# Regrouping the attention phases' exponentials: three pairs and four singles, with the PSUM banks handed out at build time

## The chip, the cores and the metric

The kernel runs on one core of a Trainium2 chip. Its engines work side by side, each through its own instructions in order: TensorE (PE) multiplies matrices into PSUM, ScalarE (ACT) computes exponentials and copies, VectorE (DVE) copies and adds, GpSimd (POOL) does small work in SBUF, and SP issues most of the DMAs. PSUM has eight banks of 128 x 512 float32; one matmul's result fills one bank. Semaphores order the engines where one needs what another has made, or where a buffer has to be free before it is written again.

The metric is the device time of one execution in microseconds, as the median of several runs. Separately, one execution was profiled instruction by instruction; times inside it are counted from its first instruction.

## What is computed

A sigmoid gate mixes two branches over one sequence of 2048 tokens and 512 channels: attention with 32 heads of 16 channels, and an MLP across the tokens.

```python
x = A_x
g = sigmoid((x * gate_w).sum(-1, keepdims=True))
# branch A: q, k, v = x @ wqkv in 32 heads of Dh = 16
scores = einsum("bhqd,bhkd->bhqk", q, k) * Dh ** -0.5
p = softmax(scores, axis=-1)
a = einsum("bhqk,bhkd->bhqd", p, v)   # heads side by side, then @ wo
# branch B: token mixing
h = layernorm(x)
u = gelu(einsum("bsd,sf->bdf", h, w1) + b1)
b = einsum("bdf,fs->bds", u, w2) + b2  # transposed back
out = g * a + (1 - g) * b
```

## The kernel before

The kernel first projects and normalizes x and computes the MLP's first layer. Then come 128 attention phases (the loop over p from line 994), and a short end that applies the output projection to the last rows.

**A phase.** Two heads and half of the queries make a group; a group takes four phases. One phase computes 16 blocks of scores, each 128 keys by 512 queries (line 1067), numbered n = 0 to 15. Each block fills one PSUM bank and is then read once from it, in one of three ways:

- a *copied* block: VectorE copies it to SBUF (line 1089), into one of six places of a wide tile; when all six are there, ScalarE takes the exponential of the whole tile, 128 x 3072, in one instruction (line 1102);
- a *single*: ScalarE takes the exponential of the one bank (line 1093);
- a *pair*: ScalarE takes the exponential of two neighbouring banks, 128 x 1024, in one instruction (line 1031, in the function exps).

Before the change, blocks 1, 3, 5, 8, 14 and 15 are copied, 0, 2, 4, 6, 7 and 9 are singles, and (10, 11) and (12, 13) are pairs.

**The second half of a phase** multiplies the exponentials with V (apply_v, line 963; "AV" below): 64 matmuls that add up in one more bank. They take first the six copied blocks of the phase before (HELD, since their wide exponential comes late) and then the ten singles and paired blocks of this phase (TURNS). VectorE adds the bank to the group's sum in SBUF (line 985). The first phase of a group ends the group before in a bank of its own, and so uses two banks in turn.

**Work beside the scores.** A score uses 64 rows of the TensorE array. Beside the first n_b scores of a phase (14 in most phases, 12 in some) stands a matmul on the other 64 rows (line 1076): a part of the MLP's second layer, of late queries or of the output projection. The scores after n_b have none, and each two of them, on different rows, can run at the same time. The list head says on which rows a score runs.

**What sets the order.** Everything here is in a manual schedule: each engine's instructions run in the order in which the program issues them. So on TensorE all 16 scores of a phase stand ahead of its AV, and AV ahead of the next phase's scores. A matmul that waits for a bank holds back all that follows it on TensorE. The extra dependencies with the reason EARLY (lines 1095, 1103, 1113) are on earlier work, so that a later instruction has one engine less to wait for. Work that other parts insert on VectorE stands in the lists amid (issued at the second to last score, line 1082) and later (after the wide exponential, line 1118).

**Banks.** One bank is kept for the matmuls beside; seven are left for the scores and AV. Before the change, the function shares turns one "spare" bank number into an order of the seven. Scores 0 to 9 are written to one-bank tiles. Then the pool is closed and opened again in another cut: two pair tiles of two banks, two one-bank tiles for scores 14 and 15, and one for AV. AV's bank, share[2], is that of score 9, the last single.

Of the kernel before, what the change touches and what calls it, by code (L numbers as in the profile page):

```python
# [9 lines left out]
F32 = mybir.dt.float32  # L10
# [22 lines left out]
NB = 512  # L33
NQ = S // NB
VC = DH + 1
SCALE = DH**-0.5
# [24 lines left out]
def gated_mix(ctx: ExitStack, tc: tile.TileContext, a_x, a_wqkv, a_wo, b_w1, b_b1, b_w2, b_b2, gate_w, out):  # L61
    nc = tc.nc
# [115 lines left out]
    with tc.tile_pool(name="vp", bufs=1, side="right") as pool:  # L178
# [138 lines left out]
        e = pool.tile([P, NS], F32, name="e")  # L317
# [4 lines left out]
        y, t, w = (pool.tile([P, NS], F32, name=n) for n in "ytw")  # L322
# [103 lines left out]
    with tc.tile_pool(name="gl", bufs=2, side="right") as gl:  # L426
# [74 lines left out]
        for f0, cs in order.items():  # L501
            n = min(NB, F - f0) // P
# [32 lines left out]
    ptp = att_ctx.enter_context(tc.tile_pool(name="pt", bufs=2, reuse_waits="tile"))  # L535
# [45 lines left out]
    PHASES, NSC, BANKS = 4, 16, 7  # L581
    LAST = NG * PHASES - 1
# [257 lines left out]
    dense = {}  # L840
# [83 lines left out]
    def shares(n):  # L924

        for one in range(0, BANKS, 2):
            lows = [k for k in range(one)][::2] + [k for k in range(one + 1, BANKS)][::2]
            for third in lows:
                if n in (third, third + 1):
                    first, second = (low for low in lows if low != third)  # L930
                    return [first, first + 1, one, second, second + 1, 2 * third + 1 - n, n]


    def regions():
        return tc.tile_pool(name="ps_s", bufs=1, space=PSUM, reuse_waits="tile")

    sums, latest, evac_done = {}, {}, []

# [49 lines left out]

    engines = {getattr(mybir.EngineType, name) for name in ("PE", "Activation", "DVE", "Pool", "SP")}
    with tc.manual_schedule(engines=engines):  # L990
        held, fence, turn, spare = [], None, 0, 0
        landed.clear()

        for p in range(LAST + 1):
# [14 lines left out]
            n_b = len(beside)  # L1009
            half = slice(0, HALF) if second else slice(HALF, P)  # L1010

            head = [second if n < n_b else (second + NSC - 1 - n) % 2 for n in range(NSC)]
            if n_b == NSC - 2:
                head[-2:] = second, 1 - second
            else:
                head[-4:] = second, 1 - second, 1 - second, second
            in_turn = list(range(n_b)) + ([14, 15] if n_b == NSC - 2 else [12, 13, 15, 14])
            qbs = {}
            for a, b in TURNS + HELD:
                if head[a] == head[b]:  # L1020
# [3 lines left out]
                    qbs[zero], qbs[one] = turn, 1 - turn  # L1024
                    turn = 1 - turn

            def exps(n):
                pt = ptp.tile([P, 2, NB], F32, name="p2", bufs=len(TWO))
                where = [share[(j - BANKS) % BANKS] for j in (n - 1, n)]
                low = min(where)  # L1030
                pairs_done.append(nc.scalar.activation(pt, twos[low, low + 1], AF.Exp, scale=SCALE))  # L1031
                for j, k in zip((n - 1, n), where):
                    units[j] = *units[j][:3], pt[:, k - low, :]

            pairs_done = []
            evac = evp.tile([P, len(EVAC), NB], F32, name="pe")
            units = {}
            share = shares(spare)
            pool = regions()
            psum = pool.__enter__()  # L1040
            ones = [psum.tile([P, NB], F32, name=f"s{n}") for n in range(BANKS)]
            for n in in_turn:
                i, qb = head[n], qbs[n]
                c = at[i][qb]
                at[i][qb] += 1
                if n < TWO[0][0]:
                    if n >= BANKS:
                        ones[share[n - BANKS]] = psum.tile([P, NB], F32, name=f"s{share[n - BANKS]}")
                    s = ones[share[n % BANKS]]
                else:  # L1050
                    if n == TWO[0][0]:
                        pool.__exit__(None, None, None)
                        pool = regions()
                        psum = pool.__enter__()
                        twos = {}
                        for low in range(BANKS):
                            if low == share[2]:
                                av = psum.tile([P, NB], F32, name="av")
                            elif low in (share[0], share[1]):
                                twos[low] = psum.tile([P, NB], F32, name=f"u{low}")  # L1060
                            elif low not in twos:
                                two = psum.tile([P, 2, NB], F32, name=f"t{low}")
                                twos[low], twos[low + 1] = two[:, 0, :], two[:, 1, :]
                                twos[low, low + 1] = two
                    s = twos[share[(n - BANKS) % BANKS]]
                rows_i = slice(i * HALF, i * HALF + ROWS)
                nc.tensor.matmul(  # L1067
                    s,
                    kt[grp][rows_i, c * P : (c + 1) * P],
                    qt[grp][rows_i, qb * NB : (qb + 1) * NB],  # L1070
                    start=True,
                    stop=True,
                )
                if n < n_b:
                    ps, a, b, begin, last, done = beside[n]
                    mm = nc.tensor.matmul(ps, a[half], b[half], start=begin and not second, stop=last and bool(second))  # L1076
                    if n == 0 and fence is not None:
                        tc.add_manual_dep(mm.ins, fence.ins.name, SYNC, reason=REASON)
                    if n == n_b - 1:
                        fence = nc.gpsimd.memset(token, 0.0)  # L1080
                        tc.add_manual_dep(fence.ins, mm.ins.name, SYNC, reason=REASON)
                if n == in_turn[-2]:
                    if n_b and second and beside[-1][-1] in between:
                        between[beside[-1][-1]]()
                    for what, *args in amid.get(p, ()):
                        what(*args)
                if n in EVAC:
                    pt = evac[:, EVAC.index(n), :]
                    nc.vector.tensor_copy(pt, s)  # L1089
                    units[n] = i, c, qb, pt  # L1090
                elif n in SINGLE:
                    pt = ptp.tile([P, NB], F32, name="p1", bufs=len(SINGLE))
                    one = nc.scalar.activation(pt, s, AF.Exp, scale=SCALE)  # L1093
                    if n == SINGLE[-1] and p:
                        tc.add_manual_dep(one.ins, earlier.ins.name, SYNC, reason=EARLY)
                    units[n] = i, c, qb, pt
                else:
                    units[n] = i, c, qb, None
                    if n in (TWO[0][1], TWO[1][1]):
                        exps(n)  # L1100
            for x in ([evac] if p < LAST else [evac[:, :2, :], evac[:, 2:, :]]):
                done = nc.scalar.activation(x, x, AF.Exp, scale=SCALE)  # L1102
# [19 lines left out]
            spare = share[2]  # L1122
            if ph == 0:
                if held:
                    apply_v(av, grp - 1, held, final=True)
                    spare = share[3]
                    av = twos[spare]
                apply_v(av, grp, turns)
            elif p < LAST:
                apply_v(av, grp, held + turns, await_loads=ph == PHASES - 1)  # L1130
            else:
                ot = sums[grp]
                nc.vector.tensor_scalar_max(ot, ot, least[0])
                first_out = ps_dn.tile([P, D], F32, name="dn")

                def meanwhile():
                    for i, (a, b) in enumerate(o_matmuls(1, NH, 0, 3)):
                        nc.tensor.matmul(first_out, a, b, start=i == 0, stop=False)

                apply_v(av, grp, held + turns + now_held, final=True, between=meanwhile)  # L1140
                last_ot = ot
            pool.__exit__(None, None, None)
            held = now_held
            if ph == PHASES - 1:
                assert at == [[NS, NS], [NS, NS]]


    with (
# [162 lines left out]
```

## Time and profile before

| What | us |
|---|---|
| Median of 3 runs (1265.22 to 1266.12) | 1265.29 |
| Span of the profiled execution, first to last instruction | 1263.6 |
| VectorE busy | 851.3 |
| Starts of the first and the last wide exponential | 283.2 and 1227.4 |

The profiled execution's time is known by its span; the three runs stand 1.6 to 2.5 us above it, for what lies before the first and after the last profiled instruction.

A line of a timeline has the start, the duration, the engine, the line of the kernel, the operation, the tiles (written <- read), their shape and how many instructions it merges; in brackets stands how long the engine was idle before and what ended that. PEld is TensorE's loading of weights, which goes on beside its matmuls. A matmul's or an exponential's recorded duration includes latency that overlaps with the next one, so the time that an engine needs for one is read from the distance of the starts or of the ends of several.

### The profile page before, as it was taken

How to read it: one execution, taken by the hardware profiler on the slowest of the kernel's cores; microseconds unless marked ns; L12 is line 12 of the kernel's file. 1: busy time of each engine (PE TensorE's matmuls, PEld its weight loads, DVE VectorE, ACT ScalarE, POOL GpSimd, SP SyncE). 2: the span in 40 equal slices, each digit the busy share in tenths (PEclk: the TensorE clock that was granted, in tenths of full speed). 3: DMA queues.
4: the chain of work that ended last, by engine and by line, in shares of the span. 5: the costliest groups of instructions: out<-in, count | busy, mean ns of one | idle time of the engine just before them, and what ended most of it. 6: DMA issues, size and time to landing. Idle time of an engine off the chain costs nothing.

```text
span 1263.6 us, 32707 instructions
## 1 busy us (share of the span) xinstructions
PE 1255.3 (99%) x13342; PEld 828.5 (66%) x13342; DVE 851.3 (67%) x1562; ACT 1069.0 (85%) x1405; POOL 198.9 (16%) x316
## 2 busy tenths in 40 slices
PE   9999999999999999999999999999999999999997
PEld 7888888875666666666666666666666666666666
DVE  5675453178767676767677677776777677678883
ACT  4443343269999999999999999999999999999990
POOL 0220444461010101010101101111111111000000
PEclk9999999999999999999999999999999999999999
DMA  4799443243744444544344443443543442366611
GB/s 132 252 333 334 145 120 105 83 129 108 214 122 104 89 102 85 157 86 97 77 105 93 97 93 84 91 88 79 114 102 71 91 100 60 56 164 177 152 59 70
DMA packets 100555, 152.31 MB, mean 121 GB/s; under 512 B 17109, under 2 KB 56171, under 8 KB 96300
## 3 DMA queue, kind: packets, MB, share of 16 engines
q1 hardware_dynamic: 99820, 149.08, 45.9%
q8 instruction: 107, 1.75, 0.6%
q10 hardware_dynamic: 576, 1.05, 0.2%
q14 instruction: 52, 0.43, 0.1%
HBM read 105.39 MB, written 44.68 MB: 119 GB/s over the span
## 4 chain that ended last, share of the span: by engine, by line
PE 99%; ACT 1%; DVE 0%; issue 0%
PE av L963 31%; PE s L1067 22%; PE acc L424 12%; PE t L1067 9%; PE acc L75 8%; PE t L963 5%; PE dn L1076 4%; PE u L1067 3%; PE pa L1162 2%; PE acc L199 1%; PE acc L268 1%; PE acc L245 0%; ACT p L1093 0%; ACT pe L1102 0%; PE dn L1162 0%; PE pa L1192 0%
## 5 line engine op out<-in xcount | busy, mean ns | idle before, releaser
L1093 ACT ACTIVATE p<-s 128x512 f32<-128x512 f32 x768 | 412.4, 791 | 0.1
L1102 ACT ACTIVATE pe<-pe 128x3072 f32<-128x3072 f32 x129 | 381.7, 2961 | 0.0
L1067 PE MATMUL s<-qs,ks 64*128 64x512 f32 x1280 | 330.2, 400 | 0.6 <-ACT p L1093 0.6
L1089 DVE COPY pe<-s 128x512 f32<-128x512 f32 x512 | 318.2, 683 | 4.8 <-PE s L1067 1.1
L1067 PEld LDWEIGHTS s<-qs,ks 64*128 64x128 f32 x1280 | 225.6, 184 | 93.3 <-issue 45.3
L1031 ACT ACTIVATE p<-t 128x1024 f32<-128x1024 f32 x256 | 278.5, 1265 | 0.0
L963 PE MATMUL av<-p,v 128*32 128x256 f32 x3880 | 227.1, 379 | 0.0
L1089 DVE COPY pe<-u 128x512 f32<-128x512 f32 x256 | 164.9, 686 | 72.0 <-PE u L1067 72.0
L963 PE MATMUL av<-pe,v 128*32 128x256 f32 x3072 | 192.5, 383 | 0.0
L985 DVE TENSOR_TENSOR ot<-av,ot 128x512 f32<-128x512 f32 (+2 forms) x160 | 93.2, 583 | 142.3 <-PE av L963 141.0
L68 POOL TENSOR_TENSOR w_lo<-w_raw,w_hi 128x512 fp32r<-128x512 f32 (+1 forms) x128 | 153.1, 1203 | 197.3 <-ACT w_hi L67 100.3
L1076 PE MATMUL dn<-u_hi,w_hi 64*128 64x512 f32 x448 | 181.1, 404 | 0.0
L963 PEld LDWEIGHTS av<-p,v 128*32 128x32 f32 x3880 | 126.0, 110 | 83.3 <-ACT p L1093 0.2
L1076 PE MATMUL dn<-u_hi,w_lo 64*128 64x512 f32 x448 | 180.6, 403 | 0.0
L1076 PE MATMUL dn<-u_lo,w_hi 64*128 64x512 f32 x448 | 180.4, 403 | 0.0
L1067 PE MATMUL t<-qs,ks 64*128 64x512 f32 x512 | 142.2, 412 | 0.0
L963 PEld LDWEIGHTS av<-pe,v 128*32 128x32 f32 x3072 | 86.7, 109 | 82.1 <-ACT p L1093 37.8
L1080 POOL MEMSET token<- 1x1 f32 x128 | 11.4, 89 | 742.2 <-PE dn L1076 701.7
L67 ACT CAST w_hi<-w_raw 128x512 fp32r<-128x512 f32 (+1 forms) x67 | 38.0, 569 | 82.9 <-PE acc L424 63.1
L1067 PEld LDWEIGHTS t<-qs,ks 64*128 64x128 f32 x512 | 72.9, 184 | 51.0 <-ACT p L1093 49.5
L424 PE MATMUL acc<-h_hi,w_hi 128*128 128x512 f32 x224 | 87.9, 392 | 0.0
L424 PE MATMUL acc<-h_hi,w_lo 128*128 128x512 f32 x224 | 87.8, 392 | 0.0
(171 smaller groups left out, 1616.0 us busy)
## 6 DMA issues: line engine op xcount, KB each, us to landing
w_raw<-in_B_w_dram SPq DMA_DIRECT2D x96, 256.0 KB
ks<-kp SPq DMA_DIRECT2D x192, 128.0 KB
qs<-qp SPq DMA_DIRECT2D x256, 64.0 KB
kp<-pc SPq DMA_DIRECT2D x16, 512.0 KB
qp<-pc SPq DMA_DIRECT2D x8, 768.0 KB
qp<-row SPq DMA_DIRECT2D x24, 256.0 KB
v<-v SPq DMA_DIRECT2D x4, 1088.0 KB
x<-in_A_x_dram SPq DMA_DIRECT2D x16, 256.0 KB
```

The lines of the kernel that those rows point to most:

```text
L67: copy(hi, src)
L68: return sub(lo, src, hi.bitcast(F32), ALU.subtract)
L75: nc.tensor.matmul(ps, a, b, start=start and n == 0, stop=stop and n == last)
L424: nc.tensor.matmul(p, a, b, start=first and k == 0, stop=last and k == 2)
L963: mm = nc.tensor.matmul(av[32 * j : 32 * (j + 1), i * QC : (i + 1) * QC], vb[b][:, v_at : v_at + 32], pt[:, h * QC : (h + 1) * QC], start= ...
L985: latest["add"] = nc.vector.tensor_tensor(x, y, x, ALU.add)
L1031: pairs_done.append(nc.scalar.activation(pt, twos[low, low + 1], AF.Exp, scale=SCALE))
L1067: nc.tensor.matmul(s, kt[grp][rows_i, c * P : (c + 1) * P], qt[grp][rows_i, qb * NB : (qb + 1) * NB], start=True, stop=True,)
L1076: mm = nc.tensor.matmul(ps, a[half], b[half], start=begin and not second, stop=last and bool(second))
L1089: nc.vector.tensor_copy(pt, s)
L1093: one = nc.scalar.activation(pt, s, AF.Exp, scale=SCALE)
L1102: done = nc.scalar.activation(x, x, AF.Exp, scale=SCALE)
```

## The change

The 16 blocks are now described by a string, one letter a block: s for a single, e for a copied block, and a, b and c for the three pairs. Blocks 0, 6, 7 and 8 are singles, 1, 4, 5, 9, 12 and 13 are copied, and (2, 3), (10, 11) and (14, 15) are pairs. The lists TURNS and HELD follow from it. The scores are issued in the order of their numbers in all phases.

The seven banks are one tile, banks, for all phases, and every access takes a slice of it. Which bank a block and AV get is worked out when the program is built: given_out goes through the 128 phases with a time for when each bank becomes free, gives each single or copied block the bank that is free first, each pair the two neighbouring banks that are free first, and AV the bank that is free first after the 16 blocks. The pair's exponential reads banks[:, low : low + 2].

```diff
-    EVAC = 1, 3, 5, 8, 14, 15
-    SINGLE = 0, 2, 4, 6, 7, 9
-    TWO = (10, 11), (12, 13)
-    TURNS = [(0, 2), (4, 6), (7, 9), *TWO]
-    HELD = [(1, 3), (5, 8), (14, 15)]
...
+    KINDS = "seaaeesssebbeecc"
+    SINGLES = 4
+    EVAC = [n for n, kind in enumerate(KINDS) if kind == "e"]
+    SINGLE = [n for n, kind in enumerate(KINDS) if kind == "s"]
+    TWO = [tuple(n for n, kind in enumerate(KINDS) if kind == two) for two in sorted(set(KINDS) - {"e", "s"})]
...
+    def given_out():
+
+        free, vector, scalar, stream, load, wide = [0.0] * BANKS, 0.0, 0.0, 0.0, 0.0, 0.0
+        given = []
+
+        def first_free(spread=1, at=None):
+            ways = [b for b in range(BANKS + 1 - spread)] if at is None else [at]
+            best = min(ways, key=lambda b: (max(free[b : b + spread]), b))
+            when = max(free[best : best + spread])
+            free[best : best + spread] = [1e9] * spread
+            return best, when
+
+        for p in range(LAST + 1):
+            singles = len(dense.get(p // 2, ()))
+            bank, open_two, scored, readers = {}, {}, {}, {}
+            copied = []
+            for n, kind in enumerate(KINDS):
+                alone = n < singles or (n - singles) % 2 == 0
+                if kind in "es":
+                    bank[n], when = first_free()
+                elif kind not in open_two:
+                    bank[n], when = first_free(2)
+                    open_two[kind] = bank[n] + 1, when
+                else:
+                    bank[n], when = open_two[kind]
+                start = max(when + 0.05, stream, load) if alone else max(when + 0.05, begun)
+                load = 0.0
+                begun, stream = start, start + 0.2305
+                scored[n] = start + 0.44
+                if kind == "e":
+                    vector = max(vector + 0.6, scored[n] + 0.69)
+                    free[bank[n]] = vector
+                    copied.append(vector)
+                elif kind == "s":
+                    scalar = max(scalar + 0.488, scored[n] + 0.6)
+                    free[bank[n]] = readers[n] = scalar
+                elif kind in readers:
+                    scalar = max(scalar + 0.914, scored[n] + 1.02)
+                    free[bank[n] - 1 : bank[n] + 1] = [scalar] * 2
+                    readers[n] = scalar
+                else:
+                    readers[kind] = None
+            done = sorted([x for x in readers.values() if x] + [readers[two[1]] for two in TWO])
+            scalar = max(scalar, max(copied) + 0.25) + 0.4267 * len(EVAC) + 0.093
+            sums = [first_free()]
+            at = max(stream + 0.12, sums[0][1])
...
+            given.append(([bank[n] for n in range(NSC)], [b for b, _ in sums]))
+        return given
...
+        given = given_out()
...
+        banks = ps_s.tile([P, BANKS, NB], F32, name="banks")
...
-            head = [second if n < n_b else (second + NSC - 1 - n) % 2 for n in range(NSC)]
-            if n_b == NSC - 2:
-                head[-2:] = second, 1 - second
-            else:
-                head[-4:] = second, 1 - second, 1 - second, second
-            in_turn = list(range(n_b)) + ([14, 15] if n_b == NSC - 2 else [12, 13, 15, 14])
+            head = [second if n < n_b else (second + n - n_b) % 2 for n in range(NSC)]
...
+            bank, av_banks = given[p]
+
+            def exps(two):
                 pt = ptp.tile([P, 2, NB], F32, name="p2", bufs=len(TWO))
...
+                low = bank[two[0]]
+                assert bank[two[1]] == low + 1
+                pairs_done.append(nc.scalar.activation(pt, banks[:, low : low + 2], AF.Exp, scale=SCALE))
...
+            av = banks[:, av_banks[0]]
+            for n in range(NSC):
...
+                s = banks[:, bank[n]]
...
-                if n == in_turn[-2]:
+                if n == NSC - 2:
...
-                    pt = ptp.tile([P, NB], F32, name="p1", bufs=len(SINGLE))
+                    pt = ptp.tile([P, NB], F32, name="p1", bufs=SINGLES)
...
-            tc.add_manual_dep(done.ins, pairs_done[0].ins.name, SYNC, reason=EARLY)
+            tc.add_manual_dep(done.ins, pairs_done[-2].ins.name, SYNC, reason=EARLY)
             evac_done.append(done)
-            earlier = pairs_done[1]
+            earlier = pairs_done[-1]
```

The functions shares and regions, the pools opened and closed in every phase and the variable spare are gone. In the first phase of a group, av is banks[:, av_banks[1]] after the group before has ended.

More of the change, by code (lines that the diff above doesn't have):

```diff
@@ L916, in gated_mix @@
     token, mark = (out_pool.tile([1, 1], F32, name=name, bufs=1) for name in ("token", "mark"))
-    EVAC = 1, 3, 5, 8, 14, 15
-    SINGLE = 0, 2, 4, 6, 7, 9
-    TWO = (10, 11), (12, 13)
-    TURNS = [(0, 2), (4, 6), (7, 9), *TWO]
-    HELD = [(1, 3), (5, 8), (14, 15)]
[L924 to L931, printed above, removed]
@@ L934, in regions @@
-    def regions():
-        return tc.tile_pool(name="ps_s", bufs=1, space=PSUM, reuse_waits="tile")
+    KINDS = "seaaeesssebbeecc"
[3 more added lines that the diff above has]
+    TWO = [tuple(n for n, kind in enumerate(KINDS) if kind == two) for two in sorted(set(KINDS) - {"e", "s"})]
+    assert all(len(two) == 2 for two in TWO) and len(KINDS) == NSC
+    own = sorted([(n, n) for n in SINGLE] + [(two[1], n) for two in TWO for n in two])
@@ new lines, in gated_mix @@
+    own = [n for _, n in own]
+    kept = list(EVAC)
+    if len(own) % 2:
+        own.remove(SINGLE[-1])
+        kept.append(SINGLE[-1])
+    TURNS, HELD = ([(x[i], x[i + 1]) for i in range(0, len(x), 2)] for x in (own, kept))
+    def given_out():
[41 more added lines that the diff above has]
+            at = max(stream + 0.12, sums[0][1])
+            at += 0.2157 * 2 * len(HELD)
+            if p % PHASES == 0 and p:
+                free[sums[0][0]] = at + 1.1
+                sums.append(first_free())
+                at = max(at, sums[1][1])
+            for i in range(0, 2 * (len(done) // 2), 2):
+                at = max(at, done[i + 1] + 0.05) + 0.2157 * 2
+            vector = max(vector + 1.6, at + 1.0)
+            free[sums[-1][0]] = vector
+            load = at + 0.3
+            given.append(([bank[n] for n in range(NSC)], [b for b, _ in sums]))
+        return given
@@ L990, in gated_mix @@
     with tc.manual_schedule(engines=engines):
-        held, fence, turn, spare = [], None, 0, 0
+        held, fence, turn = [], None, 0
+        given = given_out()
+        scores_ctx = ExitStack()
+        ps_s = scores_ctx.enter_context(tc.tile_pool(name="ps_s", bufs=1, space=PSUM, reuse_waits="tile"))
+        banks = ps_s.tile([P, BANKS, NB], F32, name="banks")
         landed.clear()
@@ L1025, in gated_mix @@
                     turn = 1 - turn
-            def exps(n):
+            bank, av_banks = given[p]
+            def exps(two):
                 pt = ptp.tile([P, 2, NB], F32, name="p2", bufs=len(TWO))
[L1029 to L1033, printed above, removed]
+                low = bank[two[0]]
+                assert bank[two[1]] == low + 1
+                pairs_done.append(nc.scalar.activation(pt, banks[:, low : low + 2], AF.Exp, scale=SCALE))
+                for k, j in enumerate(two):
+                    units[j] = *units[j][:3], pt[:, k, :]
             pairs_done = []
@@ L1037, in gated_mix @@
             units = {}
[L1038 to L1042, printed above, removed]
+            av = banks[:, av_banks[0]]
+            for n in range(NSC):
                 i, qb = head[n], qbs[n]
@@ L1045, in gated_mix @@
                 at[i][qb] += 1
[L1046 to L1065, printed above, removed]
+                s = banks[:, bank[n]]
                 rows_i = slice(i * HALF, i * HALF + ROWS)
@@ L1098, in gated_mix @@
                     units[n] = i, c, qb, None
-                    if n in (TWO[0][1], TWO[1][1]):
-                        exps(n)
+                    for two in TWO:
+                        if n == two[1]:
+                            exps(two)
             for x in ([evac] if p < LAST else [evac[:, :2, :], evac[:, 2:, :]]):
                 done = nc.scalar.activation(x, x, AF.Exp, scale=SCALE)
-            tc.add_manual_dep(done.ins, pairs_done[0].ins.name, SYNC, reason=EARLY)
+            tc.add_manual_dep(done.ins, pairs_done[-2].ins.name, SYNC, reason=EARLY)
             evac_done.append(done)
-            earlier = pairs_done[1]
+            earlier = pairs_done[-1]
             if n_b and second and beside[-1][-1]:
@@ L1121, in gated_mix @@
             turns, now_held = ([tuple(units[n] for n in pair) for pair in pairs] for pairs in (TURNS, HELD))
-            spare = share[2]
             if ph == 0:
@@ L1125, in gated_mix @@
                     apply_v(av, grp - 1, held, final=True)
-                    spare = share[3]
-                    av = twos[spare]
+                    av = banks[:, av_banks[1]]
                 apply_v(av, grp, turns)
@@ L1141, in gated_mix @@
                 last_ot = ot
-            pool.__exit__(None, None, None)
             held = now_held
@@ L1145, in gated_mix @@
                 assert at == [[NS, NS], [NS, NS]]
+        scores_ctx.close()
     with (
```

## The prediction

> **What bounds the kernel now.** I read the page first, then ScalarE's timeline over one phase, then TensorE's over the same phase, then who waits for the single exponentials. The page (busy time by engine, tenths by slice, the chain that ended last):
>
> ```profile
> span 1263.6 us, 32707 instructions
> ...
> PE 1255.3 (99%) x13342; PEld 828.5 (66%) x13342; DVE 851.3 (67%) x1562; ACT 1069.0 (85%) x1405; POOL 198.9 (16%) x316
> ...
> ACT  4443343269999999999999999999999999999990
> ...
> PEclk9999999999999999999999999999999999999999
> ...
> PE 99%; ACT 1%; DVE 0%; issue 0%
> ```
>
> The chain names TensorE, but a busy PE is no proof: matmuls overlap. ScalarE is full from the ninth slice on, in the 128 attention phases. Its timeline over one phase (start, duration, count):
>
> ```profile
> 706.88 3.01 ACT L1102 ACTIVATE pe<-pe 128x3072 f32<-128x3072 f32 x1
> 709.58 3.25 ACT L1093 ACTIVATE p<-s 128x512 f32<-128x512 f32 x6
> 712.47 2.20 ACT L1031 ACTIVATE p<-t 128x1024 f32<-128x1024 f32 x2
> 714.31 3.00 ACT L1102 ACTIVATE pe<-pe 128x3072 f32<-128x3072 f32 x1
> 717.00 0.79 ACT L1093 ACTIVATE p<-s 128x512 f32<-128x512 f32 x1
> ```
>
> Starts run ahead of the work, so I go by ends. The wide exponential ends at 706.88+3.01 = 709.89, the six singles at 712.83, the two pairs at 714.67, the next wide one at 717.31. That is 2.94 for six singles (0.49 each), 1.84 for two pairs (0.92 each), 2.64 for the wide one: 7.42 us, with every instruction started before the last one ended. **ScalarE is saturated at 7.42 us a phase.** TensorE over the same phase:
>
> ```profile
> 709.05 0.50 PE L1067 MATMUL s<-qs,ks 64*128 64x512 f32 x1
> ...
> 709.39 0.39 PE L1067 MATMUL s<-qs,ks 64*128 64x512 f32 x1
> ...
> 711.23 0.39 PE L1067 MATMUL s<-qs,ks 64*128 64x512 f32 x1
> ...
> 712.47 0.42 PE L1067 MATMUL u<-qs,ks 64*128 64x512 f32 x2
> 712.88 1.50 PE L963 MATMUL av<-pe,v 128*32 128x256 f32 x24
> 714.20 2.34 PE L963 MATMUL av<-p,v 128*32 128x256 f32 x40
> 716.47 0.49 PE L1067 MATMUL s<-qs,ks 64*128 64x512 f32 x1
> ```
>
> The first score takes 0.34 us to the second; the next eight take (711.23-709.39)/8 = 0.23 each. The last two scores, with no other matmul beside them, start together, and the product with V ("AV") 0.41 later. AV to the next phase's first score: 716.47-712.88 = 3.59. So TensorE's own loop, if no bank is late, is 0.34 + 13 x 0.23 + 0.41 + 3.59 = 7.33: **only 0.09 below ScalarE**. And AV waits for a bank even now (who waited for L1093):
>
> ```profile
>   PEld av L963: 38.1, 128
> ```
>
> AV started 0.05 after the sixth single ended (712.88 against 712.83), and this row counts such a wait in all 128 phases. It costs nothing yet, because ScalarE's backlog covers it.
>
> **What the change takes away.** Two singles become one pair: 2 x 0.49 - 0.92 = 0.06 us a phase, 7.36 in place of 7.42, 7.7 us in 128 phases. Vector copies (six), matmuls, loads and stores stay as many; nothing is added to SP's or POOL's queue. Vector work inserted between copies now comes behind the sixth copy, with some 2.5 us until the AV sum needs VectorE; I cost it at nothing; without that cover it would cost its own length in the few phases that have it. A score into half of a pair no longer waits for both banks; that is counted below, bank by bank.
>
> **What it moves.** The order becomes s e a a e e s s s e b b e e c c (s single, e copied, a/b/c pairs). Scores 14 and 15, which were copied by VectorE, are now pair c and need two neighbouring banks; TensorE works in order, so AV stands behind them. I followed the function in the diff through its 128 phases for its bank numbers alone, taking no time from it. The later of c's two banks to come free was last read by: copy 9 with single 7 in 42 phases (class A), single 8 in 59 (class B), copy 12 in 27 (class C). Phase 67's banks are 3 6 1 2 4 5 0 3 6 4 1 2 0 5 3 4 (c in 3, 4: score 7's and 9's, class A); phase 69's 4 1 5 6 2 0 3 4 1 2 5 6 3 0 1 2 (c in 1, 2: score 8's, B); phase 68's 0 5 1 2 3 4 6 0 5 3 1 2 6 4 5 6 (c in 5, 6: 12's, C).
>
> How late are these? Latencies with no backlog come from the first phase, where ScalarE starts empty, and from a phase in which the last scores came late:
>
> ```profile
> 278.57 0.39 PE L1067 MATMUL s<-qs,ks 64*128 64x512 f32 x1
> ```
> ```profile
> 279.00 0.60 ACT L1093 ACTIVATE p<-s 128x512 f32<-128x512 f32 x1
> ```
> ```profile
> 709.81 2.49 DVE L1089 COPY pe<-s 128x512 f32<-128x512 f32 x4
> 712.92 1.29 DVE L1089 COPY pe<-u 128x512 f32<-128x512 f32 x2 [0.62 <-PE u L1067]
> ```
> ```profile
> 1119.37 1.28 DVE L1089 COPY pe<-s 128x512 f32<-128x512 f32 x2
> ...
> 1120.70 0.19 PEld L1067 LDWEIGHTS u<-qs,ks 64*128 64x128 f32 x2 [0.32 <-DVE pe L1089]
> ...
> 1121.13 0.84 PE L963 MATMUL av<-pe,v 128*32 128x256 f32 x10
> ```
> ```profile
> L1031 ACT ACTIVATE p<-t x256: 1068/1281/1325, 281.4 to 1225.6; 128x1024 f32<-128x1024 f32 x128
> ```
>
> A single ends 0.43 + 0.60 = 1.03 after its score starts. A pair with nothing queued is not shown. Its floor is 0.43 + 0.92 (its service) = 1.35; its ceiling 0.43 + 1.07 (the least of 256 rows, which still had a queue) = 1.50. I take 1.03 + (0.92-0.49) = 1.46, near the ceiling, because that row is a pair itself. A copy starts 709.81-709.39 = 0.42 after its score and takes 0.69, ending 1.11 after; the next copies follow at (2.49-0.69)/3 = 0.60. A score starts 0.05 after the bank's reader ends (1119.37+1.28 = 1120.65, then 1120.70), and after such a wait AV comes 0.43 after the last score (1121.13). That step has 0.23, a score's spacing, as its other end, and I take 0.43 because that row is the same situation.
>
> From a phase's first score (0): scores 1, 3, 4, 9 and 12 at 0.34, 0.80, 1.03, 2.19 and 2.88 (9 waits 0.01 for copy 4's bank). Pair a ends at 0.80+1.46 = **2.26**: ScalarE could take it sooner, but it wants score 3. Singles 6, 7, 8 then end at 2.75, 3.24, **3.73**. Copies 4, 5 and 9 end at 2.14, 2.74 and **3.34**, and copy 12 at 2.88+1.11 = **3.99**. So:
> - A: last score 3.39, AV 3.80, next phase 3.80+3.59 = **7.39**.
> - B: 3.78 + 0.43 + 3.59 = **7.80**.
> - C: 4.04 + 0.43 + 3.59 = **8.06**.
>
> ScalarE needs 7.36 of each, so TensorE's loop sets all three. The stall stands on the path: AV, the next first score and the next pair a all come later by it, and ScalarE, ahead by then, idles.
>
> Sum against 7.42: 42 x -0.03 + 59 x 0.38 + 27 x 0.64 = -1.3 + 22.4 + 17.3 = +38.4. Two corrections. The last phase (class C) has nothing behind it but its own wide exponentials, which end where they did: -0.6. ScalarE also does two tanh beside phases 1 to 3, at most a single's 0.49 each now paid in full and mostly covered by the new idle time: -0.8. **+37.0 us: span 1263.6+37.0 = 1300.6.** The runs' median, 1265.29, stands 1.7 above the profiled span; so 1302.3.
>
> **Rivals.** *ScalarE stays the bound.* If c's banks came free by 3.33, TensorE would need 7.33 and ScalarE 7.36: 1265.3-7.7 = **1257.6** (1261.5 if every phase were class A). For it: the saturated rows. The Trainium skill, "Perfetto Trace Analysis", section Optimizing Scalar/DVE Operations, says that each operation pays a fixed access overhead (some 51 ns for ScalarE on PSUM) and that grouping into larger operations raises throughput where the engine is saturated. By it the gain would be an estimated 128 x 0.051 = 6.5 us, close to my row's. Against it: single 8 would have to end 0.4 us sooner, and in 86 phases the bank is simply handed out too late. 6%.
>
> *Whole-tile waits.* If waits were kept for the one tile and not for each bank, every score would wait for the reader before it: four singles x 1.08, six copies x 1.16, three pairs x (0.23+1.51), AV 3.59: some 20 us a phase, 1265+128x12.7 = **2890**. No row shows a tile of seven banks; against it, each access in the diff names its one or two banks. 3%.
>
> *The clock falls.* Stalls of 0.5 to 0.7 us a phase could lower TensorE's clock; at 0.9 in all phases the matmul stream of some 7.3 us adds 0.8 each: **1400**. But a longer stall is in the trace:
>
> ```profile
> 286.58 0.50 PE L1067 MATMUL s<-qs,ks 64*128 64x512 f32 x1 [0.57 <-ACT p L1093]
> ```
> ```profile
> 284.00:304.00 20.00, 19.41 (x218) 11.07 (x214) 16.68 (x30) 20.00 (x27) 2.82 (x4) 1.00 0.17 26
> ```
>
> The stretch that holds it kept clock 1.00 (third number from the end). 4%. The Trainium skill, "TensorE: Matmul & The Clock Gate", section "A second HAM failure mode: psum-queue depth-cycling", reports a kernel that cycled PSUM banks and whose clock swung between half and full rate from micro-idling; the trace above disagrees so far, for one such stretch.
>
> **How the numbers follow.** Forecast 87%, the rivals 6, 3 and 4. Measurement tells about 0.2%, 2.5 us. Faster 0.05 and same 0.01 (both the first rival), slower 0.94. Range: the unqueued pair at its floor takes 0.11 from B's 59 phases (6.5 us), AV's step at 0.23 takes 0.20 from 86 (17 us); the pair at its ceiling adds 2.4. Both low ends at once are unlikely, and uncovered work on VectorE might add some 5: 1287 to 1311.
>
> **What would show it.** Phases of three lengths, near 7.39, 7.80 and 8.06, in the classes' order; waits of scores 14 and 15 on the single exponentials (B) and copies (C), 0.45 and 0.7 us; ScalarE idle before pair a, none at AV's old wait; clock still 1.00. Wrong if phases are all 7.36, if single 8's bank stalls nobody, or if pair a ends much sooner than 2.26.

## The result, and the profile after

| | before | after |
|---|---|---|
| median, us | 1265.36 | 3846.77 (3845.62 to 3847.86) |
| profiled span, us | 1263.6 | 3846.1 |
| mean granted clock of TensorE | 1.00 | 0.648 |

The runs of before stood beside those of after on the same chip. The ratio is 3.0402, 95% interval 3.0359 to 3.0445. The forecast of 1302.3 us had the direction right and missed the time by far; the experiments below show that the delay which it had named is some 52 of the 2581 us. The page of the kernel after (span, busy time by engine, tenths in slices, the chain that ended last, the costliest group):

```profile
span 3846.1 us, 32527 instructions
...
PE 2321.4 (60%) x13342; PEld 1044.1 (27%) x13342; DVE 913.1 (24%) x1570; ACT 1156.9 (30%) x1277; POOL 197.3 (5%) x316
...
ACT  4333222232222232323232232232323232323222
...
PEclk9995656566666656666666666666666666665657
...
PE 61%; ACT 18%; DVE 16%; issue 3%; DMA 0%; SPq 0%; DVEq 0%
...
L1099 PE MATMUL banks<-qs,ks 64*128 64x512 f32 x2048 | 1291.3, 702 | 1350.4 <-DVE pe L1121 550.0
```

No engine is the bound any more. ScalarE, 9 tenths full in the attention slices before, is at 2 to 3. The chain, 99% TensorE before, now runs through ScalarE for 18% and VectorE for 16%: they take turns. The scores' group (2048 matmuls) stands behind 1350.4 us of idle TensorE. The view of waits says for whom (who waited, for whom: us in total, times, longest us):

```profile
PE banks L1099 <- DVE pe L1121: 550.0, 705, 0.8
...
PE banks L1099 <- ACT p L1125: 349.5, 512, 0.7
PE banks L1099 <- ACT p L1085: 283.8, 256, 1.1
...
PE banks L1099 <- DVE ot L1038: 116.9, 127, 1.1
...
PE banks L1099 <- DVE mark L1144: 49.1, 63, 0.8
```

That is 705 + 512 + 256 + 127 + 63 = 1663 waits, and one more stands in another row: 13 in each of 128 phases (1664). A phase has 16 scores, and the second one of each of its three pairs has nothing to wait for: **all the scores but these wait.** One phase in the timeline, from a first score to the next first score:

```profile
1000.00 0.50 PE L1099 MATMUL banks<-qs,ks 64*128 64x512 f32 x1 [0.89 <-DVE ot L1038]
...
1000.54 0.60 ACT L1125 ACTIVATE p<-banks 128x512 f32<-128x512 f32 x1 [4.60 <-PE banks L1099]
1001.19 0.50 PE L1099 MATMUL banks<-qs,ks 64*128 64x512 f32 x1 [0.69 <-ACT p L1125]
...
1001.73 0.69 DVE L1121 COPY pe<-banks 128x512 f32<-128x512 f32 x1 [1.78 <-PE banks L1099]
1002.47 0.50 PE L1099 MATMUL banks<-qs,ks 64*128 64x512 f32 x1 [0.78 <-DVE pe L1121]
...
1004.32 0.66 PE L1099 MATMUL banks<-qs,ks 64*128 64x512 f32 x1 [1.11 <-ACT p L1085]
...
1010.29 0.79 PE L1099 MATMUL banks<-qs,ks 64*128 64x512 f32 x1 [0.68 <-ACT p L1125]
...
1011.76 0.79 PE L1099 MATMUL banks<-qs,ks 64*128 64x512 f32 x1 [0.68 <-ACT p L1125]
...
1020.73 2.79 PE L1016 MATMUL banks<-pe,v 128*32 128x256 f32 x24 [1.12 <-ACT p L1085]
...
1026.61 0.69 DVE L1038 TENSOR_TENSOR ot<-banks,ot 128x512 f32<-128x512 f32 x1 [7.84 <-PE banks L1016]
1027.35 0.49 PE L1099 MATMUL banks<-qs,ks 64*128 64x512 f32 x1 [0.89 <-DVE ot L1038]
```

Score, exponential, next score; score, copy, next score. The score at 1001.19 goes to another bank than the one that was being read, and yet it starts 0.05 after the exponential of the score before has ended (1000.54 + 0.60 = 1001.14). A step is 1.19 us for a single, 1.28 for a copy (1001.19 to 1002.47) and 1.85 for a pair (1002.47 to 1004.32). From 1010.29 to 1011.76 a single's step takes 1.47 and its matmul 0.79 in place of 0.50: the granted clock has dropped. The stretches of this phase (length; busy time of PE, PEld, DVE, ACT and POOL with counts; third from the end is the clock):

```profile
1000.00:1004.30 4.30, 1.74 (x8) 0.67 (x8) 0.69 (x1) 1.62 (x2) 0.00 (x0) 1.00 0.00 0
1004.30:1018.80 14.50, 7.46 (x20) 2.70 (x20) 3.46 (x6) 2.81 (x4) 0.09 (x1) 0.51 0.00 1
1018.80:1027.30 8.50, 6.52 (x66) 2.87 (x66) 0.69 (x1) 3.68 (x2) 0.00 (x0) 0.64 0.00 0
```

Where the waits stand the clock is half; it comes back in AV, the one stretch without them (0.64 in the mean of that stretch), and the first scores of the next phase still have it (1.00).

**How much is waits, how much is clock?** An estimate from these rows: at full clock a phase would take 4 x 1.19 + 6 x 1.28 + 3 x 1.85 = 18.0, then AV's 3.59 (from the timeline of before), then 0.74 from the add at 1026.61 to the next score, 22.3 in all. (The third pair's two scores start together, which makes its step some 0.3 less, and AV's add came 3.73 after AV's start in the kernel before: 22.1 by these.) The phase took 27.35. Against 7.42 before, some 15 us a phase (1900 us in 128) are the turn-taking and some 5 (640 us) the clock. No run removed one without the other, so the split stays an estimate.

### The profile page after: what moved, and what is told of

The parts are those of the page before. It is cut to its first block, busy times and chain, and to the rows that moved or that the text cites. A ratio compares the mean times of both kernels' runs of the same rounds, so it can differ in the third digit from the quotient of the medians.

```text
span 3846.1 us, 32527 instructions
## 1 busy us (share of the span) xinstructions
PE 2321.4 (60%) x13342; PEld 1044.1 (27%) x13342; DVE 913.1 (24%) x1570; ACT 1156.9 (30%) x1277; POOL 197.3 (5%) x316
## 3 DMA queue, kind: packets, MB, share of 16 engines
q8 instruction: 106, 1.74, 0.2%
## 4 chain that ended last, share of the span: by engine, by line
PE 61%; ACT 18%; DVE 16%; issue 3%; DMA 0%; SPq 0%; DVEq 0%
PE banks L1099 34%; PE banks L1016 18%; DVE pe L1121 13%; ACT p L1085 10%; ACT p L1125 8%; PE acc L424 4%; DVE ot L1038 3%; PE acc L75 3%; PE dn L1108 1%; PE pa L1193 1%; DMA o<-ot 0%; PE acc L199 0%; PE acc L268 0%; SPq L1004 0%; DVEq L1038 0%
## 5 line engine op out<-in xcount | busy, mean ns | idle before, releaser
L1099 PE MATMUL banks<-qs,ks 64*128 64x512 f32 x2048 | 1291.3, 702 | 1350.4 <-DVE pe L1121 550.0
L1099 PEld LDWEIGHTS banks<-qs,ks 64*128 64x128 f32 x2048 | 476.3, 262 | 2163.3 <-DVE pe L1121 882.0
L1121 DVE COPY pe<-banks 128x512 f32<-128x512 f32 x768 | 530.9, 691 | 1896.7 <-PE banks L1099 1038.8
L1085 ACT ACTIVATE p<-banks 128x1024 f32<-128x1024 f32 x384 | 392.8, 1023 | 1161.1 <-PE dn L1108 641.9
L1125 ACT ACTIVATE p<-banks 128x512 f32<-128x512 f32 x512 | 305.7, 597 | 1330.7 <-PE dn L1108 1133.9
L1016 PE MATMUL banks<-pe,v 128*32 128x256 f32 x3072 | 355.8, 632 | 141.7 <-ACT p L1085 141.7
L1016 PE MATMUL banks<-p,v 128*32 128x256 f32 x5120 | 387.3, 459 | 25.6 <-DVE ot L1038 24.5
L1108 PE MATMUL dn<-u_hi,w_lo 64*128 64x512 f32 x448 | 310.4, 693 | 0.0
L1108 PE MATMUL dn<-u_lo,w_hi 64*128 64x512 f32 x448 | 308.4, 688 | 0.0
L1016 PEld LDWEIGHTS banks<-p,v 128*32 128x32 f32 x5120 | 192.0, 138 | 249.4 <-issue 135.3
```

The lines of the kernel that those rows point to most:

```text
L1016: mm = nc.tensor.matmul(av[32 * j : 32 * (j + 1), i * QC : (i + 1) * QC], vb[b][:, v_at : v_at + 32], pt[:, h * QC : (h + 1) * QC], start= ...
L1085: pairs_done.append(nc.scalar.activation(pt, banks[:, low : low + 2], AF.Exp, scale=SCALE))
L1099: nc.tensor.matmul(s, kt[grp][rows_i, c * P : (c + 1) * P], qt[grp][rows_i, qb * NB : (qb + 1) * NB], start=True, stop=True,)
```

## The experiments

Two theories at first. **T1**: nearly all of the loss comes from the packaging, seven banks as one tile, with waits kept for the tile; the new order of the blocks costs only the forecast's 37 us. **T2**: the order and the hand-out of the banks cost far more than the forecast had, and the tile has only a share.

### The change with waits bank by bank

The changed kernel, in which each access to the tile is declared free of the accesses to other banks, and each write is made to depend on the last reader of its own bank.

```diff
+    def touch(made, which, write=False, keep=None):
+        for other, theirs, wrote in on_banks:
+            if not which & theirs and other is not keep and made.ins.engine != other.ins.engine:
+                tc.declare_no_dep(made.ins, other.ins, reason=OTHER_BANK)
+        if write:
+            for b in which:
+                for other, theirs, wrote in reversed(on_banks):
+                    if b in theirs:
+                        if not wrote and made.ins.engine != other.ins.engine:
+                            tc.add_manual_dep(made.ins, other.ins.name, SYNC, reason="the bank was read")
+                        break
+        on_banks.append((made, which, write))
...
+                touch(mm, {bank[n]}, True)
```

> The changed kernel with its order, its bank numbers and its one tile, but with every wait between accesses to different banks of that tile declared unnecessary, and a wait kept only between a write to a bank and the last reads of the same bank. Theory (the one tile makes each score wait for the last reader of any bank, and the clock falls because of it): TensorE's clock is back at 1.00 and the time falls from 3846.8 to about 1302 us (phases of 7.39, 7.80 and 8.06 us, as the prediction summed them), at most 1311. Rival 1 (the bank order or the three pairs themselves cost most of it): over 2000. Rival 2 (once the waits are gone, ScalarE is the bound as planned): 1257 to 1262.

Measured: 1317.69 us, ratio 1.0418 (1.0401 to 1.0436). The page of this kernel:

```profile
span 1315.7 us, 32613 instructions
...
PE 1294.0 (98%) x13342; PEld 847.2 (64%) x13342; DVE 877.1 (67%) x1570; ACT 1087.2 (83%) x1277; POOL 198.6 (15%) x316
...
PEclk9999999999999999999999999999999999999999
```

Of the 2581 us that the change costs, 2529 go with the waits between different banks, and the clock is back with them. T1 holds in its main point; what is left is 52 us, 15 more than the forecast's 37, and the time is 7 above the bound of 1311 that was expected.

The forecast's own phases 67, 68 and 69, in the timeline of weight loads (all are scores; in brackets the idle time before and what ended it):

```profile
802.84 0.18 PEld L1119 LDWEIGHTS banks<-qs,ks 64*128 64x128 f32 x1 [0.41 <-issue]
...
810.41 0.18 PEld L1119 LDWEIGHTS banks<-qs,ks 64*128 64x128 f32 x1 [0.41 <-issue]
...
814.18 0.18 PEld L1119 LDWEIGHTS banks<-qs,ks 64*128 64x128 f32 x1 [0.50 <-ACT p L1146]
814.66 0.18 PEld L1119 LDWEIGHTS banks<-qs,ks 64*128 64x128 f32 x1 [0.30 <-DVE pe L1142]
...
818.68 0.18 PEld L1119 LDWEIGHTS banks<-qs,ks 64*128 64x128 f32 x1 [0.41 <-issue]
...
822.45 0.19 PEld L1119 LDWEIGHTS banks<-qs,ks 64*128 64x128 f32 x2 [0.40 <-ACT p L1146]
...
826.48 0.18 PEld L1119 LDWEIGHTS banks<-qs,ks 64*128 64x128 f32 x1 [0.41 <-issue]
```

Class A takes 7.57 (802.84 to 810.41), C 8.27, B 7.80, in the forecast's order. In B the last two scores wait for the single (ACT p) and start 3.77 after the first (822.45 - 818.68); in C one waits for a single and the other for a copy (DVE pe).

### The kernel before, its banks as one tile

The order, banks, singles and pairs of before; only the tiles of each phase give way to slices of one tile.

```diff
-                    s = twos[share[(n - BANKS) % BANKS]]
+                s = banks[:, share[n % BANKS] if n < TWO[0][0] else share[(n - BANKS) % BANKS]]
...
-            av = twos[spare]
+            av = banks[:, share[2]]
...
-                pairs_done.append(nc.scalar.activation(pt, twos[low, low + 1], AF.Exp, scale=SCALE))
+                pairs_done.append(nc.scalar.activation(pt, banks[:, low : low + 2], AF.Exp, scale=SCALE))
```

> The kernel before, with its order of blocks, its bank numbers, its six singles and two pairs, and only the packaging changed: the seven banks are slices of one tile instead of tiles of their own. Theory (the one tile alone makes the scores wait): as slow as the changed kernel or slower, since it has 14 reads a phase in place of 13, and each costs some 1.2 to 1.5 us: 3850 to 4050 us, clock 0.6 to 0.7. Rival (it takes the new order or the handed out banks): 1260 to 1275 us, clock 1.00.

Measured: 3987.61 us (one run beside 1264.95 of the kernel before). Its page:

```profile
span 3985.7 us, 32292 instructions
...
PE 2439.0 (61%) x13342; PEld 1089.0 (27%) x13342; DVE 907.4 (23%) x1562; ACT 1193.1 (30%) x1405; POOL 197.7 (5%) x316
...
PEclk9996565656656565666656556565555656556667
```

The packaging alone, without anything of the new order, costs more than the whole change. With two pairs in place of three, a phase has 14 scores that aren't the second of a pair, one more than after.

### The same, with waits bank by bank

The kernel above with touch on each access, as in the first experiment, and nothing else.

> The kernel before with its order of blocks and its bank numbers, its banks as slices of one tile as in the run that took 3987.6 us, but with waits bank by bank. Theory (one tile costs nothing once its waits are kept bank by bank; what the run with two pairs and handed out banks lost is its order and its hand-out): 1262 to 1268 us, within 0.2% of before, clock 1.00. Rival (one tile stays dearer, by the waits that are left or by the first score of a pair that now starts on one bank): 1275 us or more.

Measured: 1266.14 us, ratio 1.0007 (0.9998 to 1.0017).

```profile
PE 1253.5 (99%) x13342; PEld 841.0 (67%) x13342; DVE 849.8 (67%) x1562; ACT 1069.0 (85%) x1405; POOL 198.9 (16%) x316
```

The two kernels differ in waits alone: 3987.61 against 1266.14. So one tile as such costs nothing that can be measured; what costs is that its banks are waited for as one. These waits stand in the program, put there for the tile: with them declared unnecessary the same accesses take the time of before.

### What brings the clock back? Scores three times

The next two ask about the other 640 us. **C1**: the granted clock follows how busy TensorE is, so more work between the same waits brings it back, and added matmuls cost little. **C2**: it follows the waits themselves, and added matmuls cost their time at half clock. Here each score of the changed kernel is computed three times into the same bank.

```diff
-                nc.tensor.matmul(
+                for _ in range(3):
+                    nc.tensor.matmul(
```

> The changed kernel with each score's matmul issued three times into its bank, the same result each time: TensorE works two matmuls more in each of its waits. A phase of the changed kernel lasts 27.35 us, by its rows at full clock it would last 22.4 (1.19 a single, 1.28 a copy, 1.85 a pair, 4.5 for the product with V, the sum and the wait behind it). Two more matmuls cost 0.46 us a step at full clock, 13 steps a phase. Theory that the clock falls because TensorE idles: its clock comes back to 0.9 or more, a phase lasts about 28.3, and the time is 3850 to 4000 us although the work grew. Rival (the clock stays at 0.65, whatever TensorE does between the waits): two more matmuls cost 0.8 a step, 38 us a phase, 5000 to 5300 us.

Measured: 5469.32 us (one run). Its windows, the stretch of scores in one phase, columns as above:

```profile
1012.00:1045.00 33.00, 22.65 (x74) 12.09 (x78) 4.15 (x7) 6.91 (x7) 0.09 (x1) 0.50 0.00 0
```

TensorE is busy for 22.65 of 33.00 us, 69%, and the clock is 0.50. C1's forecast fails: a share of 51% in the kernel after (7.46 of 14.50) has become 69%, and the clock has not moved. A rule by the busy share with a bound above that is not excluded. The time is above C2's figure too. That figure counted two matmuls more in 13 steps, but 16 scores a phase are tripled, and a single's step became 2.33 us (1024.04 to 1026.37 in this trace) in place of 1.47.

### What brings the clock back? Work on all rows

A score uses half of the array's rows, so the clock might go by rows at work. Two matmuls over all 128 rows now stand ahead of each score, in its bank; the score overwrites them.

```diff
+                for _ in range(2):
+                    nc.tensor.matmul(
+                        s,
+                        kt[grp][:, c * P : (c + 1) * P],
+                        qt[grp][:, qb * NB : (qb + 1) * NB],
+                        start=True,
+                        stop=True,
+                    )
```

> The changed kernel with its waits for the whole tile, and ahead of each score, behind the same wait, two matmuls over all 128 rows of the array into the bank that the score then overwrites. The run with each score issued three times left the clock at 0.60 and took 40.3 us a phase; there the matmuls that were added used 64 rows. Theory (the clock follows how much of the array works, over both rows and time): the clock rises to 0.9 or more, the phase lasts 22.4 + 16 x 0.46 = 29.8 us, and the time is 4000 to 4250 us with as many matmuls as in that run. Rival (the clock stays down as long as the waits are there): 5400 to 5900 us at 0.60.

Measured: 6325.9 us (one run), above both expectations. The same two views of its scores, first the timeline, then the windows:

```profile
1042.50 1.22 PE L1100 MATMUL banks<-qs,ks 128*128 128x512 f32 x2 [0.78 <-DVE pe L1129]
1043.65 0.79 PE L1107 MATMUL banks<-qs,ks 64*128 64x512 f32 x1
```
```profile
1035.00:1070.00 35.00, 25.45 (x65) 10.44 (x68) 4.07 (x7) 6.30 (x7) 0.09 (x1) 0.50 0.02 8
```

73% busy, with the added matmuls on all rows, still 0.50. So neither these added matmuls nor the rows brought the clock back while the waits of some 0.7 to 1.1 us stayed between them. At the other end stands the kernel with waits bank by bank: some of its scores wait too, TensorE is busy for 98%, and its clock is 1.00. Between the two, neither the length and number of waits nor the busy share at which the clock drops was found, and it is open which of them it follows.

### Another order of the blocks, waits bank by bank

If the forecast's class argument is right, an order in which no pair is last should give the stall back. The first experiment with the copied blocks later and the last pair earlier:

```diff
-    KINDS = "seaaeesssebbeecc"
+    KINDS = "seaaeeesssbbcece"
```

> Waits bank by bank as in the run that took 1317.7 us, three pairs and four singles, another order of blocks: s e a a e e e s s s b b c e c e. Its pairs stand earlier and copies between them. Theory (ScalarE's 7.36 us can't be reached with seven banks, since AV and the next first score need 7.3 and any late bank adds to it; this order has the least lateness of those that I worked through): phases of 7.50 to 7.60, 1275 to 1290 us, still slower than before. Rival (the order was only badly chosen and three pairs pay as meant): 1257 to 1262 us.

Measured: 1275.84 us, ratio 1.0086 (1.0069 to 1.0103), 42 us less than the order of the change, as expected. One of its least stalled phases, weight loads (1119 the first score, 1034 AV):

```profile
707.64 0.18 PEld L1119 LDWEIGHTS banks<-qs,ks 64*128 64x128 f32 x1 [0.41 <-issue]
...
709.85 0.18 PEld L1119 LDWEIGHTS banks<-qs,ks 64*128 64x128 f32 x1 [0.29 <-DVE pe L1142]
...
711.47 1.02 PEld L1034 LDWEIGHTS banks<-pe,v 128*32 128x32 f32 x24 [0.25 <-ACT p L1146]
715.06 0.18 PEld L1119 LDWEIGHTS banks<-qs,ks 64*128 64x128 f32 x1 [0.41 <-issue]
```

715.06 - 707.64 = 7.42, the time of a phase before. Leaving out the very first phase, whose AV is shorter, the shortest in the trace takes 7.40, and their mean is 7.52. Score 9 waits for a copy's bank here (709.85), and it starts late in the shortest phase too. So no phase of this order reaches ScalarE's 7.36: TensorE's loop, with this late bank in it, takes the gain. Whether an order without a late bank exists wasn't tried.

### Two pairs and six singles, waits bank by bank, banks handed out

Numbers of pairs, singles and copies as before, so no ScalarE gain; the hand-out of given_out and an order with two singles last.

```diff
-    KINDS = "seaaeesssebbeecc"
-    SINGLES = 4
+    KINDS = "esseaaeeessebbss"
+    SINGLES = 6
```

> Waits bank by bank and banks handed out by the same function, but two pairs and six singles as before, in the order e s s e a a e e e s s e b b s s. ScalarE's sum is 7.42 again. Theory (handing out banks costs nothing by itself): 1264 to 1273 us, within 0.7% of before. Rival (one tile with waits bank by bank is itself slower than tiles of their own, through the waits or the order of release): 1290 us or more.

Measured: 1278.78 us (before beside it 1265.09), ratio 1.0109 (1.0092 to 1.0125): between the two expectations. Who waited in this kernel, and in the kernel before with one tile and waits bank by bank:

```profile
PEld banks L1119 <- DVE pe L1142: 61.3, 187, 0.4
...
PEld banks L1119 <- ACT p L1146: 3.1, 8, 1.1
```
```profile
PEld banks L1070 <- ACT p L1097: 28.8, 103, 1.0
PEld banks L1070 <- DVE pe L1093: 24.9, 104, 0.4
```

The scores wait longer for copies' banks than under the fixed plan, and less for singles': 64.4 against 53.7 us in all, so these rows do not explain the 14 us by themselves. With these two orders the banks handed out first-free are no better than the fixed ones; whether the hand-out or the order costs the 14 us wasn't separated. No kernel of the study beat the kernel before.

## Why the prediction was wrong, by its own steps

**The step that failed: "A score into half of a pair no longer waits for both banks; that is counted below, bank by bank."** The edit "banks are one tile" was priced as if waits went by bank. They went by tile: 1663 waits where the forecast had two or three a phase (score 9 and the last two). The pair of runs 3987.61 and 1266.14 shows it with nothing else changed. The forecast's ground, that each access in the diff names its banks, was true of what is read and written, and said nothing about what is waited for. A sign stood in the trace of before, and the step's own sentence names it: there a score into half of a pair waited for both banks of the pair's tile. In the phase that the forecast read, the first score of pair (10, 11) goes to the bank of copied block 3, whose copy ended at 711.10, but its weights load 0.05 after single 4, the reader of the neighbour bank, has ended at 711.36:

```profile
711.41 0.18 PEld L1067 LDWEIGHTS t<-qs,ks 64*128 64x128 f32 x1 [0.22 <-ACT p L1093]
```

A tile of two banks was already waited for as one; the forecast took that wait away by putting all seven into one tile.

**The rival that came true was also too cheap.** "Whole-tile waits" had 20 us a phase and 2890 us, with a chance of 3%. Its steps were each about 0.11 short (1.08 for a single against 1.19, 1.16 against 1.28, 1.74 against 1.85; 13 of them, 1.5 us), and it left out the wait for VectorE's add of AV (0.7): 20.0 + 1.5 + 0.7 = 22.2, the 22.3 estimated above. The rest of the phase's 27.35 is the clock: that rival's steps are all at full rate.

**The clock rival was argued away by one row, and it does not exclude the other.** The stretch quoted there had a single wait of 0.57 in 20 us and kept 1.00; that says nothing of 13 waits in one phase. The two rivals were given chances as if only one could happen; the second came with the first, and went with it. The Trainium skill, "TensorE: Matmul & The Clock Gate", section "A second HAM failure mode: psum-queue depth-cycling", which the forecast set aside, describes what came: short idle gaps between groups of matmuls, and a clock that swings between half and full. The runs agree (0.51 and 1.00 within one phase).

**Behind the packaging the forecast was close.** Its mechanism gives the direction by itself (1317.69 against 1264.95 for the kernel before), but 2529 of the 2581 us come from what it had put at 3%. With waits bank by bank its sum has a test: 1317.69 against 1302.3, above its range by 7. By class, from the first scores of the phases in that trace:

| class | phases | forecast, us | mean measured, us |
|---|---|---|---|
| A | 42 | 7.39 | 7.61 |
| B | 59 | 7.80 | 7.79 |
| C | 27 | 8.06 | 8.29 |

B, the largest class, is met (7.81 without the very first phase, which takes 6.50), and with it single 8's end, its bank, AV's 0.43 and the 3.59. A and C are 0.2 too short. TensorE's timeline of phase 67 (class A; the rows are scores 0, 8, 9 and 10, 12, and AV) shows where:

```profile
802.85 0.49 PE L1119 MATMUL banks<-qs,ks 64*128 64x512 f32 x1
...
804.78 0.39 PE L1119 MATMUL banks<-qs,ks 64*128 64x512 f32 x1
805.11 0.50 PE L1119 MATMUL banks<-qs,ks 64*128 64x512 f32 x1
805.45 0.40 PE L1119 MATMUL banks<-qs,ks 64*128 64x512 f32 x1
...
805.92 0.39 PE L1119 MATMUL banks<-qs,ks 64*128 64x512 f32 x1
...
806.82 1.50 PE L1034 MATMUL banks<-pe,v 128*32 128x256 f32 x24
```

Score 9 was to wait 0.01 for copy 4's bank and start at 2.19; it starts at 805.11 - 802.85 = 2.26. And score 10 comes 0.34 behind it, not the 0.23 of a running stream: the step that the forecast had seen behind a phase's first score stands behind this one too, which had to wait. So score 12 starts at 3.07 (forecast 2.88) and AV at 3.97 (3.80): A is late by its scores, C by copy 12, which follows score 12. B's last scores wait for a single in ScalarE's chain, and that does not move. The terms that were mis-sized are thus score 9's wait and the step behind it: 42 x 0.22 + 27 x 0.23 - 59 x 0.01 = 14.9 of the 15.4 us.

**ScalarE's gain of 7.7 us** never showed. The forecast's reason, that TensorE's loop is next, held, and so did the 7.33 that it gave this loop. The kernel before with one tile and waits bank by bank has a phase of 7.33 (1036.09 - 1028.76), in which no score comes later than the stream's step (0.34 behind the first, then 0.23):

```profile
1028.76 0.18 PEld L1070 LDWEIGHTS banks<-qs,ks 64*128 64x128 f32 x1 [0.41 <-issue]
...
1036.09 0.18 PEld L1070 LDWEIGHTS banks<-qs,ks 64*128 64x128 f32 x1 [0.41 <-issue]
```

In the two regrouped orders that were run with waits bank by bank, some score came late in every phase; that no order can reach 7.36 isn't shown.

## What to carry to other kernels

Before you price an edit that only repackages buffers, find out per what the waits are kept: look in a trace whether a write waits for readers of other parts of the same buffer. When a rival puts a wait between every two steps of an engine, price it whole: the step from end to start with its latency, the work at the phase's end that nothing hides any more, and the clock under that pattern. And put last in the order a block that any one buffer will do for, not one that needs two neighbours to be free (1275.84 against 1317.69 here, though these two orders differ in other places too).

## What was unexpected of the hardware

The granted clock fell although TensorE was never idle for long. The longest wait of the scores in the kernel after was 1.1 us (PE rows of the waits), and the longest of AV 1.4; yet the clock was 0.51 over 14.5 us, and with 69% and with 73% of the stretch busy it was 0.50. The Trainium skill, "TensorE: Matmul & The Clock Gate", section "HAM oscillation — how this bites in real kernels", puts the rule as no idle gaps above some 3.4 us; here gaps of some third of that, repeated, went with half rate, so the measurement goes before that rule. By the times at which the granted clock changes in the trace of the kernel after, half rate mostly lasts 20.5 us (103 of 129 times) and full rate 6.8, over and over; with the 128-row matmuls added, where a phase is longer, half rate most often lasts 41.0 (54 of 126 times). In the attention phases of the kernel after, full rate came back within AV, the one unbroken stream of matmuls in a phase, in 127 of 128 times, in the median 3.8 us after its start; it was lost again in the median some 4 us after a phase's first score.
